# Small bias and gate loads behind the x^T loads, and the K weights in two held halves, in a fused attention and token-MLP kernel

## The chip, the cores and the metric

The kernel runs on one core of one Trainium2 chip. The metric is the device time of one execution in microseconds (us). Before the change the median of five runs is 165.92 us (165.42 to 166.23).

## What is computed

Two mixers read the same x (2048 tokens x 512 features, bf16), and a gate per token blends them:

```
g = sigmoid(sum(x * gate_w))              # one number per token
a = attention(x)                          # 32 heads of 16; each token sees itself and the tokens
                                          # 2, 4, ... 14 back (8 places); then @ wo
h = layernorm(x)                          # over features
u = gelu(einsum("bsd,sf->bdf", h, w1) + b1)   # mixes over the 2048 tokens, F = 1792
b = einsum("bdf,fs->bds", u, w2) + b2         # back to 2048 tokens
out = g * a + (1 - g) * b
```

## The kernel before, in words

All memory on chip is one arena, cut into named regions; `ps` is the accumulator memory of 8 banks. The work has these stages:

1. Head. TensorE warms up on constants (line 546). Token block 0 of x (tiles 0 to 3) is loaded tile by tile, turned on TensorE (line 562), copied out by VectorE (line 574) and ScalarE, and multiplied with Wq, whose four quarters come one by one (line 583), into banks 0 to 3. Between the Q matmuls stand three small transposes (lines 599 to 601): b1, the gate vector and b2 were loaded as rows of 14, 4 and 16 partitions side by side (views `B1R`, `GWR`, `B2R` of the region ROWS) and are turned into columns in bank 7. VectorE copies them out (lines 612 to 614).
2. Projections (line 650), four matmuls of 512 columns each: K and V of block 0, Q and K of block 1, Q and K of blocks 2 and 3, then V of blocks 1 to 3. Blocks 1 to 3 of x^T come by transposing DMAs (`ld_xt`, line 490). ScalarE evacuates the banks, which go round in a ring of seven that leaves out bank 3.
3. Beside this, VectorE takes layer norm statistics (line 682), normalises x (line 696), and forms the attention products Q x K (line 449 is the helper for nearly all of VectorE's work). In the first half of the tokens two additions of such products are done by accumulating DMAs on POOL's queue (`qaddd`, line 737).
4. TensorE sweeps w1 (line 848; two halves of 8 matmuls for each of 14 tiles of F), and between two such halves it forms gate and logit sums over the products (lines 707 and 712). Softmax and the weighted sums over V go on VectorE until near the end.
5. TensorE sweeps w2 (line 875) and adds the output projection of attention (line 884), which needs VectorE's finished blocks `ot0` to `ot7`, two tiles each. ScalarE blends and SP stores.

The order of every engine is set by a planner (`_Sched`): each operation is added with its engine, an estimated duration, what it reads and writes, and a priority; the planner runs through time, takes for each engine the ready operation that can start first, and among equals the one with the longest remaining chain plus its priority. TensorE's operations are chained in the order in which they are written, apart from the logit sums, which go where the planner finds them ready. The waits are then set from the dependences. Loads on one queue are chained in the order in which they are written (`load`, `last_ld`), so a load that waits holds back all that follow it on its queue. SP's queue carries, in this order: x0, Wq0, x2, Wq2, Wk, Wv, x4-7, x^T 1, x8-11, x^T 2, x12-15, x^T 3, the first slab of w1, and then slabs that wait for others. ScalarE's queue carries x1, Wq1, x3, Wq3. POOL's queue carries the gate vector, b1 and b2, later the accumulating DMAs.

Of the kernel before, what the change touches and what calls it, by code (L numbers as in the profile page):

```python
# [5 lines left out]
BF16 = mybir.dt.bfloat16  # L6
# [7 lines left out]
D = 512  # L14
# [4 lines left out]
NST = S // 128  # L19
NFT = F // 128  # L20
# [260 lines left out]
class _Mem:  # L281
# [17 lines left out]
    def view(self, name, dtype, dims, extra=0, p0=0, np_=128):  # L299
        base = self.arena[:].bitcast(dtype)  # L300
        pst = base.ap[0][0]
        esz = mybir.dt.size(dtype)
        o = self.off[name]
        assert o % esz == 0
        return bass.AP(base.tensor, p0 * pst + o // esz + extra, [[pst, np_]] + [list(d) for d in dims])


def bass_gated_mix__sliding_local_dilated__mixer_token_mlp__prompt_kernel(nc, A_x, A_wqkv, A_wo, B_x, B_w1, B_b1, B_w2, B_b2, gate_w, out, dbg=None):
    with contextlib.ExitStack() as es:
        block = es.enter_context(nc.Block())  # L310
        m = _Mem(nc, es)
# [23 lines left out]
        m.region("OUTS", 5 * D * 2)  # L335
        m.region("RP", 32 * 2)
        m.region("GWREP", 4 * 32 * 2)
        m.region("ROWS", 384 * 2)
        m.region("MASK", NW * PAD * 2)
        m.region("SMALL", 2048)  # L340
        m.alias("UT", "WQKV")
# [4 lines left out]
        view = m.view  # L346
# [3 lines left out]
        A = sch.add  # L350

        x2d = A_x[0]
        xv = x2d.rearrange("(t p) d -> p t d", p=128)
        wqkv_v = A_wqkv.rearrange("(dt p) c -> p dt c", p=128)
# [5 lines left out]
        XT = view("XT", BF16, [(S, 4), (1, S)])  # L360
        UT = view("UT", BF16, [(D, NFT), (1, D)])
        WQKV = view("WQKV", BF16, [(3 * D, 4), (1, 3 * D)])
# [37 lines left out]
        IDENT = view("IDENT", BF16, [(1, 128)])  # L400
        ONES = view("ONES", BF16, [(1, 128)])
        RP = view("RP", BF16, [(1, 32)])
        GWREP = view("GWREP", BF16, [(32, 4), (1, 32)])
        MASK = view("MASK", BF16, [(PAD, NW), (1, PAD)], np_=32)
        B1R = view("ROWS", BF16, [(1, 128)], np_=NFT)
        B2R = view("ROWS", BF16, [(1, 128)], extra=128, np_=NST)
        GWR = view("ROWS", BF16, [(1, 128)], extra=256, np_=4)
        so = [0]

        def small(n, dims=None, extra=0):  # L410
# [20 lines left out]
        B1C = small(NFT)  # L431
        B2C = small(NST)
# [5 lines left out]
        def psb(bank):  # L438
            return ps[:, bank, :].bitcast(BF16)

        def sub(ap_, offs, dims):
            return bass.AP(ap_.tensor, ap_.offset + offs, [list(ap_.ap[0])] + [list(d) for d in dims])
# [12 lines left out]
        GELU = "gelu_apprx_tanh_and_others"  # L455
# [6 lines left out]
        A("pool", lambda e: e.memset(sub(KH[0], 0, [(KR, 4), (1, PAD)]), 0.0), 0.2, writes=["kpad"], name="kpad")  # L462
        A("pool", lambda e: e.memset(sub(V5, 0, [(VR, 4), (1, PAD)]), 0.0), 0.2, writes=["vpad"], name="vpad")

        def f_mask(e):
            ins = None
            for w in range(NW):
                if w:
                    ins = e.memset(psub(MASK, 0, 32, w * PAD, [(1, 2 * w)]), NEG)
                if 2 * w < PAD:  # L470
                    ins = e.memset(psub(MASK, 0, 32, w * PAD + 2 * w, [(1, PAD - 2 * w)]), 0.0)
            return ins
# [12 lines left out]
        def load(name, dst, src, nbytes, writes, transpose=False, queue="sp", issue=0.5, order=True, deps=(), after=()):  # L485
            ds = sch.dsem(name)

            def fn(e):
                if transpose:
                    return e.dma_start_transpose(dst, src)  # L490
                return e.dma_start(dst, src)  # L491
            op = sch.dma(queue, fn, nbytes, ds, issue=issue, writes=writes, deps=list(deps) + late_dep[0],
                         after=list(after) + ([last_ld[queue]] if order and queue in last_ld else []), name=name)
            if order:
                last_ld[queue] = op
            return op
# [5 lines left out]
            load(name, WQKV[:, d0:d1, tn * D:(tn + 1) * D], wqkv_v[:, d0:d1, tn * D:(tn + 1) * D], (d1 - d0) * 128 * D * 2, [res])  # L502

        def ld_xt(sb):
            load("xT%d" % sb, XT[:, :, sb * 512:(sb + 1) * 512], x2d[sb * 512:(sb + 1) * 512, :], int(1.4 * 512 * D * 2), ["xt%d" % sb],
                 transpose=True, issue=3.3)

        def ld_first(name, dst, src, nbytes, res, queue):
# [2 lines left out]
        def xq(t, queue):  # L511
            return ld_first("x%d" % t, X[:, t:t + 1, :], xv[:, t:t + 1, :], 131072, ["x%d" % t], queue)

        def wqq(k_, queue):
            return ld_first("wq%d" % k_, WQKV[:, k_:k_ + 1, 0:D], wqkv_v[:, k_:k_ + 1, 0:D], 131072, ["wq%d" % k_], queue)

        for k_ in (0, 2):
            xq(k_, "sp")
            xq(k_ + 1, "act")
            wqq(k_, "sp")  # L520
            wqq(k_ + 1, "act")
        load("wk", WQKV[:, 0:4, D:2 * D], wqkv_v[:, 0:4, D:2 * D], 4 * 128 * D * 2, ["wk"])
        load("gw", GWR, gate_w.rearrange("(t p) -> t p", p=128), 1024, ["gwr"], issue=0.6, queue="pool")
        load("b1", B1R, B_b1.rearrange("(t p) -> t p", p=128), 4096, ["b1r"], issue=0.6, queue="pool")
        load("b2", B2R, B_b2.rearrange("(t p) -> t p", p=128), 4096, ["b2r"], issue=0.6, queue="pool")
        ld_w("wv", 2, 0, 4, "wv")
        for k_ in range(1, 4):
            ld_x(4 * k_, 4)
            ld_xt(k_)

        def ld_w1(j):
            w1ld[j] = load("w1_%d" % j, W1H[j], w1v[:, :, 256 * j:256 * j + 256], S * 256 * 2, [W1R[j]] + (XTALL if j in (3, 4) else []), order=j < 3,
# [18 lines left out]
        def PE(fn, dur, reads, writes, name, prio=0):  # L551
            op = A("pe", fn, dur, reads=reads, writes=writes, after=([chain[0]] if chain[0] is not None else []), name=name, prio=prio)
            chain[0] = op
            return op
# [41 lines left out]
               "q0_%d_%d" % (hb, dt))  # L596

        def f_tb(e):
            e.transpose(out=psb(7)[:, 512:512 + NFT], in_=B1R, identity=IDENT[0:NFT, 0:NFT])  # L599
            e.transpose(out=psb(7)[:, 576:580], in_=GWR, identity=IDENT[0:4, 0:4])  # L600
            return e.transpose(out=psb(7)[:, 544:544 + NST], in_=B2R, identity=IDENT[0:NST, 0:NST])  # L601

        pe_tx(0)
        pe_q0(0, 0)
# [3 lines left out]
        pe_q0(1, 0)  # L608
        pe_q0(1, 1)
        pe_q0(1, 2)  # L610
        PE(f_tb, 0.17, ["b1r", "b2r", "gwr", "ident"], ["b7"], "t_b12")
        A("dve", lambda e: e.tensor_copy(out=GWREP, in_=sub(psb(7), 576, [(1, 4), (0, 32)])), 0.2, reads=["b7"], writes=["gwrep"], name="gwrep", prio=-20)
        A("dve", lambda e: e.tensor_copy(out=B1C, in_=psb(7)[:, 512:512 + NFT]), 0.15, reads=["b7"], writes=["b1c"], name="b1c", prio=-20)
        A("dve", lambda e: e.tensor_copy(out=B2C, in_=psb(7)[:, 544:544 + NST]), 0.15, reads=["b7"], writes=["b2c"], name="b2c", prio=-20)
        pe_q0(2, 3)
        XT0 = ["xt0_%d_%d" % (t, k_) for t in range(4) for k_ in range(2)]

# [23 lines left out]
        def bank_():  # L641
            b = ring[1][ring[0] % len(ring[1])]
            ring[0] += 1
            return b

        def f_proj(tn, dl, sb, bank):
            def fn(e):
                ins = None
                for dt in range(4):
                    ins = e.matmul(ps[:, bank, :], lhsT=sub(WQKV, dt * 3 * D + tn * D + dl, [(4, 128)]),  # L650
                                   rhs=XT[:, dt, sb * 512:(sb + 1) * 512], start=(dt == 0), stop=(dt == 3))
                return ins
            return fn

        WR = {0: ["wq0", "wq1", "wq2", "wq3"], 1: ["wk"], 2: ["wv"]}

        def proj(tn, dl, sb):
            bank = bank_()
            PE(f_proj(tn, dl, sb, bank), 0.87, xt_res(sb) + WR[tn], ["b%d" % bank], "pj%s%d_%d" % ("qkv"[tn], dl, sb))
            evac(tn, dl, sb, bank)  # L660

        for dl in range(4):
            proj(1, dl, 0)
        for dl in range(4):
            proj(2, dl, 0)
        for dl in range(4):
# [3 lines left out]
          reads=["k%d_1" % dl for dl in range(4)], writes=["khalo"], name="khalo")  # L670
        for dl in range(4):
            for tn in range(2):
                for sb in (2, 3):
                    proj(tn, dl, sb)
        ring[0], ring[1] = 0, [0, 1, 2]
        for dl in range(4):
            for sb in range(1, 4):
# [3 lines left out]
        for t in range(NST):  # L681
            A("dve", (lambda t_: lambda e: e.bn_stats(out=ST6[:, t_, :], in_=X[:, t_, :]))(t), 0.67,  # L682
              reads=["x%d" % t], writes=["st%d" % t], name="st%d" % t, prio=-20, after=[extl["dve"]])
# [37 lines left out]
        for h in range(2):  # L721
# [13 lines left out]
            def qaddd(x_, y_, s_, h=h):  # L735
                o_, i_ = (sub(PB[b_], s_ * 4096, [(1, 4096)]) for b_ in (x_, y_))
                qkd[h, s_] = sch.dma("pool", lambda e: e.dma_start(o_, i_, accum_op=ALU.add, max_dma_last_dim=4096), 1800000, sch.dsem("qd%d_%d" % (h, s_)),  # L737
                                     issue=1.3, reads=[PS[y_][s_]], writes=[PS[x_][s_]], name="qd%d_%d" % (h, s_))

            for s_ in range(2):  # L740
                qk(0, bb[0], s_)
# [112 lines left out]
        for ft in range(NFT):  # L854
            bank = MLPB[ft]
            for half in range(2):
                PE(f_ph2(ft, bank, half), 1.735, ["x%d" % t for t in range(8 * half, 8 * half + 8)] + [W1R[ft // 2]], ["b%d" % bank],
                   "ph2_%d_%d" % (ft, half))
            A("act", act(UT[:, ft, :], ps[:, bank, :], AF.Gelu_apprx_tanh, bias=col(B1C, ft)), 0.7,
              reads=["b%d" % bank, "b1c"], writes=["ut%d" % ft] + (["wq0", "wq1", "wq2", "wq3", "wk", "wv"] if ft == 0 else []), name="gel%d" % ft, table=GELU)  # L860
            if ft % 2 == 1 and ft // 2 + 5 <= 6:
                ld_w1(ft // 2 + 5)
        for j in range(8):
# [145 lines left out]
```

## Time and profile before

| | us |
|---|---|
| median of five runs | 165.92 (165.42 to 166.23) |
| the profiled execution's own time | 165.87 |
| its span, first to last instruction | 164.1 |
| TensorE busy | 159.2 |
| VectorE busy | 150.8 |
| ScalarE busy | 75.4 |
| first K matmul (line 650) starts | 9.81 |
| first accumulating DMA issued on POOL | 18.79 |
| first slab of w1 issued on SP | 19.68 |
| logit sums of the first half (line 707) start | 53.14 |

The granted TensorE clock is 1.0 in the whole run. In the profile a line of the timeline gives the start in the span, the time, the engine, the line of the kernel, the operation with output and input, the count, and in brackets how long the engine was idle before it and what released it. Neighbours of one form are merged into one line. "PEld" is TensorE's weight load, which runs beside the matmul before it. A line of the windows gives, for a stretch of time, the busy time and count of PE, PEld, DVE (VectorE), ACT (ScalarE) and POOL, then the granted clock, the share of the 16 DMA engines and the rate in GB/s. The chain is followed back from the last instruction, at each step to what released it.

### The profile page before, as it was taken

Reading aid. Unit: us, or ns where it says so; the run is one execution under the profiler, and the core shown is the slowest. Engines: PE = TensorE matmul, PEld = TensorE weight load, DVE = VectorE, ACT = ScalarE, POOL = GpSimd, SP = SyncE. Lnnn points to the kernel's source line nnn. Section 1 sums busy time; section 2 is a strip of 40 time slices with the busy share of each in tenths; the row PEclk is TensorE's granted clock in tenths of the full one; section 3 lists DMA queues with packets and bytes.
Section 4 is the critical chain, followed back from the end, with each engine's and each line's share of the span. In section 5 each row is a group of like instructions: output and inputs, shape, how many; then the busy total and the mean of one; then the engine's idle time right before and its main releaser. Section 6 shows DMA issues by size and latency. Waiting matters only on the chain.

```text
span 164.1 us, 1993 instructions
## 1 busy us (share of the span) xinstructions
PE 159.2 (97%) x795; PEld 77.3 (47%) x810; DVE 150.8 (92%) x126; ACT 75.4 (46%) x104; POOL 13.7 (8%) x38
## 2 busy tenths in 40 slices
PE   7999999999999999999999999999999999999993
PEld 3755555555544444444444344444444444444641
DVE  0589999999999999999999999999999999999940
ACT  3356677666773599952211669210121111111164
POOL 7000300020000000005000000005001222000000
PEclk9999999999999999999999999999999999999999
DMA  4999999439399287999998974995994899970014
GB/s 160 285 314 268 219 222 216 113 59 187 69 306 279 63 214 212 293 289 265 182 232 241 275 202 138 295 237 148 276 230 149 175 209 191 204 180 35 32 56 136
DMA packets 44696, 32.24 MB, mean 196 GB/s; under 512 B 7952, under 2 KB 42256, under 8 KB 44688
## 3 DMA queue, kind: packets, MB, share of 16 engines
q1 hardware_dynamic: 41360, 22.06, 50.3%
q0 software_dynamic: 2608, 9.45, 29.0%
q10 hardware_dynamic: 720, 0.62, 1.2%
q8 instruction: 6, 0.10, 0.2%
q14 instruction: 2, 0.02, 0.0%
HBM read 18.88 MB, written 2.10 MB: 128 GB/s over the span
## 4 chain that ended last, share of the span: by engine, by line
PE 94%; DMA 3%; ACT 1%; issue 1%; SPq 0%
PE ps L848 29%; PE ps L875 29%; PE ps L650 23%; PE ps L884 8%; DMA arena<-in_A_x_dram 3%; PE ps L583 2%; PE ps L712 1%; ACT arena L452 1%; PE ps L707 1%; SPq L491 0%; PE ps L562 0%; PE ps L599 0%; PE ps L601 0%; PE ps L600 0%
## 5 line engine op out<-in xcount | busy, mean ns | idle before, releaser
L449 DVE TENSOR_TENSOR arena<-arena 128x4096 bf16<-128x4096 bf16 (+8 forms) x79 | 132.1, 1720 | 1.5 <-ACT arena L452 0.5
L875 PE MATMUL ps<-arena 128*128 128x512 bf16 (+2 forms) x234 | 50.0, 366 | 0.2
L452 ACT ACTIVATE arena<-ps,arena 128x512 bf16<-128x512 f32 (+1 forms) x30 | 21.8, 731 | 59.1 <-PE ps L884 40.9
L848 PE MATMUL ps<-arena 128*128 128x512 bf16 x218 | 48.5, 379 | 0.3
L452 ACT ACTIVATE arena<-ps 128x512 bf16<-128x512 f32 (+3 forms) x53 | 33.0, 629 | 18.6 <-PE ps L650 10.8
L650 PE MATMUL ps<-arena 128*128 128x512 bf16 x173 | 38.0, 379 | 0.2
L875 PEld LDWEIGHTS ps<-arena 128*128 128x128 bf16 x238 | 22.8, 98 | 25.9
L848 PEld LDWEIGHTS ps<-arena 128*128 128x128 bf16 x224 | 21.7, 98 | 26.9 <-ACT arena L452 0.7
L650 PEld LDWEIGHTS ps<-arena 128*128 128x128 bf16 x176 | 19.9, 113 | 18.1
L884 PE MATMUL ps<-arena 128*128 128x512 bf16 (+2 forms) x67 | 15.6, 366 | 0.1
L944 ACT ACT_TABLE_LOAD x11 | 14.1, 1283 | 2.9 <-issue 2.7
L780 POOL DMA_DIRECT2D arena<-arena x8 | 4.3, 561 | 74.2 <-DVE arena L449 74.2
L884 PEld LDWEIGHTS ps<-arena 128*128 128x128 bf16 x68 | 6.5, 98 | 7.3
L682 DVE BATCH_NORM_STATS2 arena<-arena 128x6 f32<-128x512 bf16 x16 | 9.9, 678 | 0.0
L452 ACT ACTIVATE arena<-arena 128x16 f32<-128x16 f32 (+5 forms) x10 | 6.8, 679 | 6.1 <-DVE arena L449 6.0
L696 DVE TENSOR_SCALAR arena<-arena 128x512 bf16<-128x512 bf16 x16 | 5.3, 408 | 0.0
L817 POOL DMA_DIRECT2D arena<-arena x3 | 3.6, 1200 | 19.0 <-DVE arena L449 19.0
L574 DVE COPY arena<-ps 128x256 bf16<-128x256 bf16 x4 | 1.2, 292 | 4.2 <-PE ps L562 4.1
L737 POOL DMA_DIRECT2D arena<-arena x2 | 2.5, 1234 | 28.8 <-DVE arena L449 28.8
L583 PE MATMUL ps<-arena 128*128 128x256 bf16 (+1 forms) x27 | 3.8, 286 | 0.4 <-issue 0.2
L924 DVE TENSOR_SCALAR arena<-ps,arena 128x128 bf16<-128x128 f32 x1 | 0.4, 410 | 3.9 <-PE ps L884 3.9
L546 PE MATMUL ps<-const-bfloat16-1.0 128*128 128x512 bf16 (+1 forms) x9 | 2.7, 484 | 0.9 <-PEq L994 0.9
(35 smaller groups left out, 19.1 us busy)
## 6 DMA issues: line engine op xcount, KB each, us to landing
arena<-in_B_w_dram SPq DMA_DIRECT2D x7, 1024.0 KB, 9.3
arena<-in_B_w_dram SPq DMA_DIRECT2D x8, 896.0 KB, 8.2
arena<-arena POOLq DMA_DIRECT2D x5, 1024.0 KB, 9.2
arena<-arena POOLq DMA_DIRECT2D x8, 512.0 KB, 10.6
out_dram<-arena SPq DMA_DIRECT2D x15, 128.0 KB, 1.7
arena<-in_A_x_dram SPq DMA_DIRECT2D x3, 512.0 KB, 4.8
arena<-in_A_wqkv_dram SPq DMA_DIRECT2D x2, 512.0 KB, 6.2
arena<-in_A_wo_dram SPq DMA_DIRECT2D x1, 512.0 KB, 8.4
```

Of the source, the lines that this page charges most:

```text
L449: return lambda e: e.tensor_tensor(out=o_, in0=a_, in1=b_, op=op_)
L452: return lambda e: e.activation(out=o_, in_=i_, func=f_, **kw)
L583: ins = e.matmul(ps[:, dl, c0:c1], lhsT=sub(WQKV, dt * 3 * D + dl, [(4, 128)]), rhs=XT[:, dt, c0:c1], start=(dt == 0 and hb == 0), stop=(d ...
L650: ins = e.matmul(ps[:, bank, :], lhsT=sub(WQKV, dt * 3 * D + tn * D + dl, [(4, 128)]), rhs=XT[:, dt, sb * 512:(sb + 1) * 512], start=(dt = ...
L682: A("dve", (lambda t_: lambda e: e.bn_stats(out=ST6[:, t_, :], in_=X[:, t_, :]))(t), 0.67, reads=["x%d" % t], writes=["st%d" % t], name="s ...
L696: A("dve", (lambda t_: lambda e: e.tensor_scalar(out=X[:, t_, :], in0=X[:, t_, :], scalar1=col(RSTD, t_), scalar2=col(NMR, t_), op0=ALU.mu ...
L780: prev = sch.dma("pool", (lambda d_, s_: lambda e: e.dma_start(d_, s_))(dst, src), 524288, sch.dsem("av%d_%d" % (h, c)), issue=1.0, reads= ...
L817: sch.dma("pool", (lambda o_, i_: lambda e: e.dma_start(o_, i_, accum_op=ALU.add, max_dma_last_dim=4096))(pw(0, 4), pw(4, 4)), 1800000, sc ...
L848: ins = e.matmul(ps[:, bank, :], lhsT=W1H[ft // 2][:, st, 128 * (ft % 2):128 * (ft % 2) + 128], rhs=X[:, st, :], start=(st == 0), stop=(st ...
L875: ins = e.matmul(ps[:, bank, 0:c1 - c0], lhsT=W2S[i // 2][:, ft, 128 * (i % 2):128 * (i % 2) + 128], rhs=UT[:, ft, c0:c1], start=(ft == 0) ...
L884: ins = e.matmul(ps[:, bank, 0:c1 - c0], lhsT=OT[:, i // 2, dl, 128 * (i % 2):128 * (i % 2) + 128], rhs=WO[:, dl, c0:c1], start=False, sto ...
L944: e.preload_act_table_set(want)
```

## The change

The region ROWS shrinks to one row of 128 per partition, and the three vectors lie below each other, b1 from partition 0, b2 from 16, the gate from 32; POOL clears the region first. Their loads move from POOL's queue to SP's, behind x^T 3 and ahead of the first slab of w1. One transpose of the whole 128 x 128 region takes the place of the three; it goes to bank 3 and stands after the second column group (dl = 1) of the Q and K projections of blocks 2 and 3. VectorE's three copies move with it. Wk is loaded in two halves, both of which wait until x0 has landed; for the first two column groups of K, block 0, the matmuls of the first half of the depth are done for both before those of the second. The first accumulating DMAs wait for x^T 3 (`deps=[xtld]`).

```diff
-        m.region("ROWS", 384 * 2)
+        m.region("ROWS", 128 * 2)
...
+        ROWS = view("ROWS", BF16, [(1, 128)])
         B1R = view("ROWS", BF16, [(1, 128)], np_=NFT)
-        B2R = view("ROWS", BF16, [(1, 128)], extra=128, np_=NST)
-        GWR = view("ROWS", BF16, [(1, 128)], extra=256, np_=4)
+        B2R = view("ROWS", BF16, [(1, 128)], p0=16, np_=NST)
+        GWR = view("ROWS", BF16, [(1, 128)], p0=32, np_=4)
...
+        rows0 = A("pool", lambda e: e.memset(ROWS, 0.0), 0.15, name="rows0", prio=-90)
...
+        xld = {}
         for k_ in (0, 2):
-            xq(k_, "sp")
+            xld[k_] = xq(k_, "sp")
             xq(k_ + 1, "act")
             wqq(k_, "sp")
             wqq(k_ + 1, "act")
-        load("wk", WQKV[:, 0:4, D:2 * D], wqkv_v[:, 0:4, D:2 * D], 4 * 128 * D * 2, ["wk"])
-        load("gw", GWR, gate_w.rearrange("(t p) -> t p", p=128), 1024, ["gwr"], issue=0.6, queue="pool")
-        load("b1", B1R, B_b1.rearrange("(t p) -> t p", p=128), 4096, ["b1r"], issue=0.6, queue="pool")
-        load("b2", B2R, B_b2.rearrange("(t p) -> t p", p=128), 4096, ["b2r"], issue=0.6, queue="pool")
+        for k_ in range(2):
+            load("wk%d" % k_, WQKV[:, 2 * k_:2 * k_ + 2, D:2 * D], wqkv_v[:, 2 * k_:2 * k_ + 2, D:2 * D], 2 * 128 * D * 2, ["wk%d" % k_], deps=[xld[0]])
         ld_w("wv", 2, 0, 4, "wv")
         for k_ in range(1, 4):
             ld_x(4 * k_, 4)
-            ld_xt(k_)
+            xtld = ld_xt(k_)
+        load("gw", GWR, gate_w.rearrange("(t p) -> t p", p=128), 1024, ["gwr"], issue=0.4, deps=[rows0])
+        load("b1", B1R, B_b1.rearrange("(t p) -> t p", p=128), 4096, ["b1r"], issue=0.4, deps=[rows0])
+        load("b2", B2R, B_b2.rearrange("(t p) -> t p", p=128), 4096, ["b2r"], issue=0.4, deps=[rows0])
...
         def f_tb(e):
-            e.transpose(out=psb(7)[:, 512:512 + NFT], in_=B1R, identity=IDENT[0:NFT, 0:NFT])
-            e.transpose(out=psb(7)[:, 576:580], in_=GWR, identity=IDENT[0:4, 0:4])
-            return e.transpose(out=psb(7)[:, 544:544 + NST], in_=B2R, identity=IDENT[0:NST, 0:NST])
+            return e.transpose(out=psb(3)[:, 512:640], in_=ROWS, identity=IDENT)
...
-        PE(f_tb, 0.17, ["b1r", "b2r", "gwr", "ident"], ["b7"], "t_b12")
...
-        for dl in range(4):
+        kb0 = [bank_() for dl in range(2)]
+        for k_ in range(2):
+            for dl in range(2):
+                PE(f_proj(1, dl, 0, kb0[dl], 2 * k_, 2 * k_ + 2), 0.44, XT0 + ["wk%d" % k_], ["b%d" % kb0[dl]], "pjk%d_0_%d" % (dl, k_))
+                if k_ == 1:
+                    evac(1, dl, 0, kb0[dl])
+        for dl in range(2, 4):
             proj(1, dl, 0)
...
             for tn in range(2):
                 for sb in (2, 3):
                     proj(tn, dl, sb)
+            if dl == 1:
+                PE(f_tb, 0.06, ["b1r", "b2r", "gwr", "ident"], ["b3"], "t_b12")
...
-                                     issue=1.3, reads=[PS[y_][s_]], writes=[PS[x_][s_]], name="qd%d_%d" % (h, s_))
+                                     issue=1.3, reads=[PS[y_][s_]], writes=[PS[x_][s_]], deps=[xtld], name="qd%d_%d" % (h, s_))
```

The three copies of VectorE that follow the transpose read bank 3 instead of bank 7 and are otherwise the same.

More of the change, by code (lines that the diff above doesn't have):

```diff
@@ L504, in ld_xt @@
         def ld_xt(sb):
-            load("xT%d" % sb, XT[:, :, sb * 512:(sb + 1) * 512], x2d[sb * 512:(sb + 1) * 512, :], int(1.4 * 512 * D * 2), ["xt%d" % sb],
+            return load("xT%d" % sb, XT[:, :, sb * 512:(sb + 1) * 512], x2d[sb * 512:(sb + 1) * 512, :], int(1.4 * 512 * D * 2), ["xt%d" % sb],
                  transpose=True, issue=3.3)
@@ L610, in bass_gated_mix__sliding_local_dilated__mixer_token_mlp__prompt_kernel @@
         pe_q0(1, 2)
-        PE(f_tb, 0.17, ["b1r", "b2r", "gwr", "ident"], ["b7"], "t_b12")
-        A("dve", lambda e: e.tensor_copy(out=GWREP, in_=sub(psb(7), 576, [(1, 4), (0, 32)])), 0.2, reads=["b7"], writes=["gwrep"], name="gwrep", prio=-20)
-        A("dve", lambda e: e.tensor_copy(out=B1C, in_=psb(7)[:, 512:512 + NFT]), 0.15, reads=["b7"], writes=["b1c"], name="b1c", prio=-20)
-        A("dve", lambda e: e.tensor_copy(out=B2C, in_=psb(7)[:, 544:544 + NST]), 0.15, reads=["b7"], writes=["b2c"], name="b2c", prio=-20)
         pe_q0(2, 3)
@@ L644, in bank_, with f_proj @@
             return b
-        def f_proj(tn, dl, sb, bank):
+        def f_proj(tn, dl, sb, bank, d0=0, d1=4):
             def fn(e):
                 ins = None
-                for dt in range(4):
+                for dt in range(d0, d1):
                     ins = e.matmul(ps[:, bank, :], lhsT=sub(WQKV, dt * 3 * D + tn * D + dl, [(4, 128)]),
@@ L653, in f_proj @@
             return fn
-        WR = {0: ["wq0", "wq1", "wq2", "wq3"], 1: ["wk"], 2: ["wv"]}
+        WR = {0: ["wq0", "wq1", "wq2", "wq3"], 1: ["wk0", "wk1"], 2: ["wv"]}
         def proj(tn, dl, sb):
@@ L674, in bass_gated_mix__sliding_local_dilated__mixer_token_mlp__prompt_kernel @@
                     proj(tn, dl, sb)
+            if dl == 1:
+                PE(f_tb, 0.06, ["b1r", "b2r", "gwr", "ident"], ["b3"], "t_b12")
+                A("dve", lambda e: e.tensor_copy(out=GWREP, in_=sub(psb(3), 544, [(1, 4), (0, 32)])), 0.2, reads=["b3"], writes=["gwrep"], name="gwrep", prio=-20)
+                A("dve", lambda e: e.tensor_copy(out=B1C, in_=psb(3)[:, 512:512 + NFT]), 0.15, reads=["b3"], writes=["b1c"], name="b1c", prio=-20)
+                A("dve", lambda e: e.tensor_copy(out=B2C, in_=psb(3)[:, 528:528 + NST]), 0.15, reads=["b3"], writes=["b2c"], name="b2c", prio=-20)
         ring[0], ring[1] = 0, [0, 1, 2]
@@ L859, in bass_gated_mix__sliding_local_dilated__mixer_token_mlp__prompt_kernel @@
             A("act", act(UT[:, ft, :], ps[:, bank, :], AF.Gelu_apprx_tanh, bias=col(B1C, ft)), 0.7,
-              reads=["b%d" % bank, "b1c"], writes=["ut%d" % ft] + (["wq0", "wq1", "wq2", "wq3", "wk", "wv"] if ft == 0 else []), name="gel%d" % ft, table=GELU)
+              reads=["b%d" % bank, "b1c"], writes=["ut%d" % ft] + (["wq0", "wq1", "wq2", "wq3", "wk0", "wk1", "wv"] if ft == 0 else []), name="gel%d" % ft, table=GELU)
             if ft % 2 == 1 and ft // 2 + 5 <= 6:
```

## The prediction

> **What bounds the kernel now.** I read the page first: TensorE's busy row and the chain that ended last.
>
> ```profile
> PE 159.2 (97%) x795; PEld 77.3 (47%) x810; DVE 150.8 (92%) x126; ACT 75.4 (46%) x104; POOL 13.7 (8%) x38
> ...
> PE 94%; DMA 3%; ACT 1%; issue 1%; SPq 0%
> ```
>
> TensorE carries 94% of the chain. The DMA's 3% is one wait of 4.38 us from 1.73, for a tile of x. From the first K matmul on (line 650, 9.81 us) the chain shows only breaks of 0.05 us. So an edit pays only by moving the end of that head, or costs by opening a hole behind it. Next, the timeline of TensorE over the first 10 us (start, busy, and idle before it with its releaser):
>
> ```profile
> 4.89 1.04 PE L583 MATMUL ps<-arena 128*128 128x256 bf16 x8
> 6.16 0.69 PE L562 MATMUL ps<-arena 128*128 128x128 bf16 x8 [0.23 <-DMA arena<-in_A_x_dram]
> 6.88 1.94 PE L583 MATMUL ps<-arena 128*128 128x256 bf16 x16
> 8.76 0.18 PE L599 MATMUL ps<-arena 14*128 14x14 bf16 x1
> ...
> 9.16 0.81 PE L583 MATMUL ps<-arena 128*128 128x512 bf16 x3 [0.18 <-issue]
> 9.81 0.38 PE L650 MATMUL ps<-arena 128*128 128x512 bf16 x1
> ```
>
> Three losses lie there. (1) The 8 Q matmuls from 4.89 step at 0.108 us, so the array was free at 4.89 + 8 x 0.108 = 5.76; the transposes of x tiles 2 and 3 began at 6.15: 0.39 waiting for x. (2) The weight load of the next Q matmul waited for Wq's third quarter: 0.21, in the waits table ("PEld ps L583 <- DMA arena<-in_A_wqkv_dram: 0.2"). (3) The 16 Q matmuls from 6.88 are through at 6.88 + 16 x 0.108 = 8.61; the last Q group's first weight load starts at 8.91 and its first matmul (of four, one record is missing) at 9.81 - 4 x 0.216 = 8.95. The three small transposes cost 0.33, about half of it before the first of them. Then the windows, to see why x comes late (last column GB/s, before it the DMA share):
>
> ```profile
> 3.00:4.00 1.00, 0.83 (x8) 0.59 (x7) 0.00 (x0) 1.00 (x1) 1.00 (x17) 1.00 1.06 361
> 4.00:5.00 1.00, 0.86 (x10) 0.63 (x8) 0.58 (x2) 0.60 (x3) 0.03 (x1) 1.00 1.02 292
> 5.00:6.00 1.00, 0.92 (x8) 0.66 (x7) 0.00 (x0) 0.17 (x1) 0.00 (x0) 1.00 0.68 160
> ```
>
> By 5.0 us 15 + 245 + 361 + 292 = 913 KB had moved, and x0-x3, Wq0-3 together are 1,049 KB. Yet x2 landed at 1.73 + 4.4 = 6.13, x3 at 6.34, Wq2 and Wq3 at 6.8 and 7.0. Whole Wk (issued 2.64), Wv, x4-7 and the three small loads of POOL's queue were in flight beside them, and from 5 to 6 the rate fell to 160.
>
> **Removing the small transposes from the head.** Gain 0.33, as (3).
>
> **The first loads without company.** SP issues x0, Wq0, x2, Wq2, then waits until x0 has landed (0.82 + 2.8 = 3.62), and only then Wk's halves, Wv, x4-7. POOL issues nothing. If 136 KB remain at 5.0 and go at 292 to 361 GB/s, they have moved at 5.4 to 5.5; x2 comes before them, so near 5.2, and Wq3 near 5.8, allowing 0.4 for landing. TensorE would then never wait: 0.39 + 0.21 = 0.60. Bounds: 0 if the dip at 5-6 us has another cause, 0.60 at most, since TensorE is busy up to 5.76. A loss I exclude here: these eight issues stay first on SP and ACT. I take 0.60, because a transfer of the same 128 KB landed in 2.8 to 3.1 us where only others of its kind were in flight, and in 4.4 to 4.8 where Wk was.
>
> **The hold, and who stands behind it on SP.** Wk moves from 2.64 to about 3.7 and 4.15, Wv 4.6, x4-7 5.1, x^T 1 5.6 (before 4.26). Needs: K would start at 9.81 - 0.93 = 8.88; the second half is needed 2 x 0.43 later, 9.75. Whole Wk took 5.7 us under load; that gives 9.4 for the first half, if a half took as long, and 9.85 for the second: bounds 0 and 0.5. I take 0, since at 5.5 the queue ahead of it is empty and 512 KB at 361 GB/s need 1.5 us: landing near 7.5. The Trainium skill ("DMA: Bandwidth & Descriptors", under "Measured (HBM→SBUF, 128 partitions, SWDGE, issued from GpSimd)") speaks against splitting: batch to 1 MiB or more; its fit is a fixed 2.0 us plus bytes/436e3. Wholly in series that is 2 x 2.6 us, and the second half lands near 8.9, still in time; by the row of overlapped 128 KB transfers the fixed part is paid once. Either way 0. Then x^T 1: its issue lasted 6.76 us, to 11.02, against 3.39 and 3.89 for the next two, so it was waiting behind queued bytes; those are no more than before. It landed at 13.06; needed at 8.88 + 8 x 0.867 = 15.8: cover 2.7, against a hold of 1.35. x^T 3 landed at 15.74 + 6.0 = 21.7; needed 9 projections later, 23.6: cover 1.9. Without cover each microsecond late would be a microsecond of TensorE.
>
> **First accumulating DMA behind x^T 3.** POOL issued it at 18.79; now near 21.7. Behind it on POOL is only the second one (34.07), which waits for VectorE anyway. It took 9.2 us: landing 31 instead of 28. VectorE's first overwrite of its source comes at about 38: cover 7. Cost 0.
>
> **Bias and gate loads on SP.** Three issues of 0.4 to 0.5 ahead of W1's first slab: 19.68 becomes about 21. That slab took 11.4 us, beside the accumulation; 33 to 34 is far from its use at 48 less 0.7. The small ones landed in 4.0 to 5.3 us: 24 to 26.5; a row of the DMA view shows that SP's queue (q1) crawls while the accumulation (q0) runs, here from 22 to 23:
>
> ```profile
> q0 software_dynamic: 46, 0.19, 97.3%
> q1 hardware_dynamic: 38, 0.02, 9.5%
> ```
>
> 34 rows and their completions are two such microseconds, so 27 at the latest. They are used at 8.88 + 24 x 0.867 = 29.7: cover 3. Cost 0.
>
> **The full transpose in the projections.** One weight load (0.10 to 0.11) and 128 columns. Nearest row: eight such transposes from 6.16 in 0.69, 0.086 apiece, plus the 0.15 of waits that stood before the old ones, partly under a 0.216 matmul now. The skill ("TensorE: Matmul & The Clock Gate", "Part 4: PE-mode transpose") gives 275 ns in a kernel and 390 alone. By the row 0.1 to 0.25, by the page 0.28 to 0.39, which would eat the 0.33 of (3). I take 0.20: the row is this kernel's own. Bounds 0.06 and 0.4.
>
> **VectorE.** Its three copies leave 9.02-9.48, where it waited 0.32 for ScalarE afterwards, and come back near 30, where it has no idle: +0.45. The interleaved K halves finish the first K tile 0.43 later from K's start, so its first product begins 0.93 - 0.43 = 0.5 earlier. Net about 0. Its deadlines, from single rows of its timeline:
>
> ```profile
> 49.40 2.28 DVE L449 TENSOR_TENSOR arena<-arena 128x4096 bf16<-128x4096 bf16 x1
> ...
> 157.00 0.69 DVE L449 TENSOR_TENSOR arena<-arena 128x1024 bf16<-128x1024 bf16 x1
> ```
>
> The logit sums (line 707, 53.14) need the product ended at 51.68: slack 1.46, less 0.73 leaves 0.7; where the planner puts the sums one half-sweep later, it grows by 1.7 and nothing waits. The last attention block ends at 157.69, needed by the output projection of tile 14 at 156.35 + 16 x 0.216 = 159.8: slack 2.1, less 0.73 leaves 1.4. POOL's memset of the rows and its earlier small memsets lie beside waiting engines: 0.
>
> **Sum.** -0.33 - 0.60 + 0.20 = -0.73. The profiled execution took 165.87 (span 164.1 and 1.77 around it): 165.14. It stands 0.05 below the median 165.92: 165.2.
>
> **Rivals.** *x2 is late anyway* (0.29): the dip at 5-6 us belongs to the transfers themselves. Then only -0.33 + 0.20 = -0.13: 165.8, or with half of the gain 165.5. For it: between 5 and 6 us the two hardware queues still moved 0.07 and 0.09 MB, little of it Wk. Against: the quiet first four loads. That is also the case that the hold doesn't do what it says. *The held queue comes late* (0.15, the slower side): K's second half at its start on TensorE, about 9.75. If it lands as Wv did (3.2 + 6.7, under load) plus a slow start, 4.15 + 7.5 = 11.65, the stall is 1.9 against 0.73: +1.2, 167.1. It decides against the change from a landing at 10.5, and is slower by over 0.3% from 11.0. Against: half the bytes are ahead of it. *More than the sum* (0.04): the new transpose is hidden whole, 165.0. The likeliest, 165.2, has 0.52.
>
> **Chances.** 0.3% is 0.5 us, about what a measurement of this kernel can tell from no change. Faster: 0.52 + 0.04, less the part of the first case above 165.42 (0.05), plus the best of the late-x2 case (0.04): 0.55. Slower: 0.14, the held queue but for a short stall. Within: the rest, 0.31. The likeliest case alone runs from 165.0 to 165.5 by the transpose's bounds. The range goes from 164.9 (0.93 off, no price for the transpose) to 166.2, over the late x2 and a stall of K of about 1 us.
>
> **What would show it.** Right: x2's landing before 5.8 and no idle by DMA before the second group of line 562; the first K matmul near 8.9; one transpose near 30 with a hole of no more than 0.25; breaks of 0.05 elsewhere. Wrong: idle of line 650 released by a DMA of wqkv near 9.7 or of x near 16 or 24; a pause at the transpose for the b loads; VectorE as releaser of line 707 or 884.

## The result, and the profile after

Over 36 executions the changed kernel has a median of 165.49 us (164.69 to 166.47), beside 166.06 for 71 of the kernel before; the ratio is 0.9948, 95% interval 0.9932 to 0.9964, so about 0.86 us (0.60 to 1.13) were gained. Ratios here and below leave out the executions more than 1.5% above the fastest of their kernel, while medians, means and counts above 167 us are over all. The prediction said 165.2, that is 0.72 less. The size is right. This section and the next show that its largest term was not where the time came from.

The profiled execution has a span of 163.5 us against 164.1. TensorE's timeline over the head, as it was shown of before (start, busy, idle before and releaser):

```profile
4.53 1.04 PE L588 MATMUL ps<-arena 128*128 128x256 bf16 x8 [0.38 <-ACT arena L453]
5.40 0.28 PE L567 MATMUL ps<-arena 128*128 128x128 bf16 x2
5.87 0.51 PE L567 MATMUL ps<-arena 128*128 128x128 bf16 x6 [0.19 <-DMA arena<-in_A_x_dram]
6.47 2.80 PE L588 MATMUL ps<-arena 128*128 128x256 bf16 x19
9.11 3.19 PE L649 MATMUL ps<-arena 128*128 128x512 bf16 x14
```

The first K matmul comes at 9.11 instead of 9.81. The Q matmuls now run through without the three small transposes (one group of 19; one record is missing). The transposes of x tiles 2 and 3 (line 567) started at 5.40 (their weight loads at 5.29), but the third still waited for x3 until 5.87, and the Q group behind them for Wq2 until 6.47. The late transpose, from the chain of the changed kernel:

```profile
19.25 10.74 PE ps L649 x49
29.99 0.06 PE ps L604
30.05 0.05 issue
30.10 10.74 PE ps L649 x49
```

It takes 0.06 us of the chain; the 0.05 behind it stands at every 49th matmul in both kernels. From 30 us on everything is 0.65 earlier than before: nothing behind the head gives it back. In this one pair of profiles all of the gain lies in the head. That is a single execution of each, and it misleads, as the runs below show.

### The profile page after: what moved, and what is told of

It is laid out like the page before. It is cut to its first block, busy times and chain, and to the rows that moved or that the text cites. A ratio compares the mean times of both kernels' runs of the same rounds, so it can differ in the third digit from the quotient of the medians.

```text
span 163.5 us, 1989 instructions
## 1 busy us (share of the span) xinstructions
PE 158.6 (97%) x793; PEld 77.0 (47%) x808; DVE 150.7 (92%) x126; ACT 70.1 (43%) x100; POOL 12.0 (7%) x36
## 4 chain that ended last, share of the span: by engine, by line
PE 93%; DMA 3%; ACT 1%; SPq 1%; issue 1%
PE ps L858 30%; PE ps L885 29%; PE ps L649 23%; PE ps L894 8%; DMA arena<-in_A_wqkv_dram 3%; PE ps L588 2%; PE ps L722 1%; ACT arena L453 1%; SPq L494 1%; PE ps L717 1%; PE ps L604 0%
## 5 line engine op out<-in xcount | busy, mean ns | idle before, releaser
L885 PEld LDWEIGHTS ps<-arena 128*128 128x128 bf16 x238 | 22.8, 98 | 25.9
L858 PEld LDWEIGHTS ps<-arena 128*128 128x128 bf16 x224 | 21.6, 98 | 26.9 <-issue 0.8
L649 PEld LDWEIGHTS ps<-arena 128*128 128x128 bf16 x176 | 19.9, 113 | 18.0
L894 PEld LDWEIGHTS ps<-arena 128*128 128x128 bf16 x68 | 6.5, 98 | 7.3
L588 PEld LDWEIGHTS ps<-arena 128*128 128x128 bf16 x28 | 2.9, 114 | 1.0 <-DVE arena L579 0.5
```

What stands on the lines that cost most here:

```text
L588: ins = e.matmul(ps[:, dl, c0:c1], lhsT=sub(WQKV, dt * 3 * D + dl, [(4, 128)]), rhs=XT[:, dt, c0:c1], start=(dt == 0 and hb == 0), stop=(d ...
L858: ins = e.matmul(ps[:, bank, :], lhsT=W1H[ft // 2][:, st, 128 * (ft % 2):128 * (ft % 2) + 128], rhs=X[:, st, :], start=(st == 0), stop=(st ...
L885: ins = e.matmul(ps[:, bank, 0:c1 - c0], lhsT=W2S[i // 2][:, ft, 128 * (i % 2):128 * (i % 2) + 128], rhs=UT[:, ft, c0:c1], start=(ft == 0) ...
L894: ins = e.matmul(ps[:, bank, 0:c1 - c0], lhsT=OT[:, i // 2, dl, 128 * (i % 2):128 * (i % 2) + 128], rhs=WO[:, dl, c0:c1], start=False, sto ...
```

## The experiments

Ratios are to the kernel before, which ran beside each on the same chip, with 95% intervals. The runs were made in four series: the pair of the result, and three series of experiments, each on one chip with the kernel before. The kernel before has a tail: 38 of its 283 executions in the four series took over 167 us (16 of 71, 6 of 62, 10 of 75 and 6 of 75), and its mean is 166.17 where its median is 165.97. Landing times come from the one profiled execution of each run.

**The hold alone.** The kernel before with Wk in two held halves, and with the interleaved K halves (the edit is shown in part):

```diff
-        load("wk", ...4 rows of WQKV..., ["wk"])
+        for k_ in range(2):
+            load("wk%d" % k_, ...2 rows..., ["wk%d" % k_], deps=[xld[0]])
```

> The kernel before with one part of the change alone: Wk in two halves that wait for x0, with the interleaved K halves; bias and gate loads stay on POOL's queue and the three small transposes in the head. Theory (Wk and what follows it crowd the first loads): x3 lands near 5.8 and Wq2 near 6.4, as in the changed kernel, and the first K matmul starts near 9.4, so -0.4 us against before (ratio 0.9976). Rival (the three small loads on POOL's software queue are what slows the first loads): x2 still lands near 6.1, Wq2 near 6.8, first K matmul near 9.8, ratio 1.000.

Measured: 1.0016 (0.9996 to 1.0037), 5 of 22 above 167, mean 166.75. x2 landed at 5.7 and Wq2 at 6.6, between the two theories, and the first K matmul started at 9.78. The profiled execution (span 167.9) is one of the long ones and brought something else: x^T 3 landed at 26.45, and TensorE waited 2.0 us for it by the waits view.

**The change without the hold.** `deps=[xld[0]]` removed from the changed kernel.

> The changed kernel with the hold taken away: Wk's halves are issued at once; the small loads stay behind x^T 3. Theory (Wk crowds the first loads): x2 and Wq2 late again, 6.1 and 6.8; only the 0.3 of the small transposes is kept, first K matmul near 9.5, ratio to before 0.9985. Rival (POOL's small loads slowed the first loads): x2 near 5.0, Wq2 near 6.4 as in the changed kernel, first K matmul near 9.1, ratio 0.995.

Measured: 0.9967 (0.9948 to 0.9985) in 9 executions, mean 165.47. x2 landed at 5.1, x3 at 5.4, Wq2 at 6.2, earlier than with the hold. My theory that Wk crowds the first loads fell. The rival, POOL's small loads, stood for the moment.

**A longer hold.** Wk's halves wait for x2 (`deps=[xld[2]]`).

> The changed kernel with a longer hold: Wk's halves wait for x2 instead of x0, so they are issued near 5.1 and 5.5 and everything behind them on SP's queue 1.4 us later. Theory (what is left of the head's waits, 0.36 for x3 and 0.27 for Wq2 in the changed kernel, comes from Wk's first half beside them): x3 near 5.5, Wq2 near 5.9, K ready to start near 8.7; Wk's first half lands near 8.2 to 8.5, so no stall: -0.3 against the changed kernel, ratio to before 0.993. Rival (the held queue comes late): Wk's halves land after 8.9 and 9.3 and TensorE waits at K; as the changed kernel or slower, up to 1.0, with idle released by a DMA of wqkv before the K matmuls.

Measured: 1.000 (0.9983 to 1.0017), mean 166.13. Even with Wk and all that follows it held back until x2 had landed, x2 came at 5.6 and Wq2 at 6.3. The windows of this run show the queue running dry behind the hold (the last two columns are DMA share and GB/s):

```profile
5.00:6.00 1.00, 1.00 (x6) 0.68 (x5) 0.00 (x0) 0.16 (x1) 0.00 (x0) 1.00 0.41 137
6.00:7.00 1.00, 1.00 (x13) 0.86 (x12) 0.21 (x1) 0.10 (x1) 0.00 (x0) 1.00 0.17 20
```

K itself didn't wait. But x^T 1 landed at 7.67 + 8.3 = 15.97 with 16.5 as its need, and x^T 3 at 18.36 + 5.9 = 24.26 with 24.3: the cover of 2.5 and 1.9 us that the changed kernel has in its profile is used up. The held queue comes late, as the rival said, with x^T rather than K as the transfer at the edge; that it is this that costs the 0.7 us on average, the one profile does not show.

**Eight transposes in place of one.**

```diff
-            return e.transpose(out=psb(3)[:, 512:640], in_=ROWS, identity=IDENT)
+            for r_ in range(8):
+                ins = e.transpose(out=psb(3)[:, 512:640], in_=ROWS, identity=IDENT)
+            return ins
```

> The changed kernel with the whole-region transpose done eight times over in place of once: the price of one by itself. By the row of the head's transposes (0.086 each) seven more cost 0.6 us, by the Trainium skill's 275 ns 1.9 us, and by the 390 ns of a transpose alone 2.7 us. First K matmul at 9.1 as in the changed kernel; ratio to the kernel before 0.9985, 1.006 or 1.011.

Measured: 0.9992 (0.9972 to 1.0011). In its chain:

```profile
30.23 0.45 PE ps L605 x8
```

In this chain seven more cost 0.45 - 0.06 = 0.39, 0.056 each, which is about a quarter of a 512-column matmul at 0.216: the transpose in this running stream costs the time of its 128 columns and no more. By the times the seven cost somewhat more: the mean is 166.00 against 165.45 for the changed kernel over two other series, 0.55 with a standard error of 0.09. The 275 and 390 ns that the Trainium skill's "TensorE: Matmul & The Clock Gate" gives ("Part 4: PE-mode transpose") are much too large as a price in this stream by either measure (the profile records each transpose as 0.219 us long, but they overlap). My 0.20 for one was too large by the chain's 0.06.

**The change without the wait for x^T 3.** `deps=[xtld]` removed.

> The changed kernel without the accumulating DMA's wait for x^T 3. Theory (the held SP queue issues x^T 3 some 0.3 us later, and the accumulation, issued near 18.3, starves it, as in the run with the hold alone, where x^T 3 landed at 26.45 and TensorE stood still for about 3 us): in a good part of the executions x^T 3 lands after 24 and TensorE waits 1 to 3 us; several runs above 167 us, mean ratio to before above 1.000. Rival (the wait does nothing, as the prediction had it): as the changed kernel, no run above 167, ratio 0.995.

Measured: 1.0035 (1.0004 to 1.0066), 12 of 22 above 167, up to 169.99, mean 167.37, which is 1.3 above the kernel before beside it. Without the wait that I had booked at zero, the change is a loss. The accumulating DMA and x^T 3 in the timelines of this run, each in its own:

```profile
18.76 1.32 POOL L747 DMA_DIRECT2D arena<-arena  x1 [16.54 <-DVE arena L450]
```

```profile
17.32 4.64 SPq L493 DMA_TRANSPOSE arena<-in_A_x_dram  x1
```

From 24 to 25 us the DMA view has this one line for the queues, of POOL's software queue; SP's queue with x^T 3 moved no packet at all:

```profile
q0 software_dynamic: 48, 0.20, 98.4%
```

x^T 3 landed 9.7 us after its issue began, at 27.0, and not after 5.9 as with the wait. The DMA view's lines for it, the first of this run, the second of the changed kernel:

```profile
arena<-in_A_x_dram SPq DMA_TRANSPOSE x1, 9.7
arena<-in_A_x_dram SPq DMA_TRANSPOSE x1, 5.9
```

TensorE's timeline names the DMA of x as what ended its idle time:

```profile
27.11 7.64 PE L649 MATMUL ps<-arena 128*128 128x512 bf16 x28 [2.82 <-DMA arena<-in_A_x_dram]
```

The windows show what it did to TensorE (first pair after the window's length: TensorE busy; the column after POOL is the granted clock):

```profile
24.00:25.00 1.00, 0.29 (x2) 0.00 (x0) 0.96 (x6) 0.97 (x4) 0.00 (x0) 1.00 0.98 197
25.00:26.00 1.00, 0.00 (x0) 0.00 (x0) 1.00 (x1) 0.25 (x2) 0.00 (x0) 1.00 0.99 197
26.00:27.00 1.00, 0.00 (x0) 0.00 (x0) 0.96 (x3) 0.00 (x0) 0.00 (x0) 0.82 1.34 259
27.00:28.00 1.00, 0.89 (x3) 0.36 (x4) 1.00 (x4) 0.00 (x0) 0.00 (x0) 0.50 0.84 202
28.00:29.00 1.00, 1.00 (x4) 0.37 (x3) 1.00 (x5) 0.00 (x0) 0.00 (x0) 0.50 1.15 347
29.00:30.00 1.00, 1.00 (x3) 0.29 (x2) 1.00 (x5) 0.60 (x1) 0.00 (x0) 0.50 1.19 295
```

TensorE idles for 2.8 us. Its granted clock falls to half while it still idles (0.82 for the window from 26 to 27, so from about 26.6) and stays there until 30.0: seven matmuls at 0.427 instead of 0.216, 1.5 us more. This stall of 2.8 us costs 4.3.

**The kernel before with that wait alone** (the lines that set `xtld` are left out here).

```diff
-                issue=1.3, reads=[PS[y_][s_]], writes=[PS[x_][s_]], name=...
+                issue=1.3, reads=[PS[y_][s_]], writes=[PS[x_][s_]], deps=[xtld], name=...
```

> The kernel before with the wait for x^T 3 alone. Theory (the kernel before sometimes meets the same collision, which is its tail of runs above 167 us: 16 of 71 and 6 of 62, against none of 36 of the changed one): the tail goes, the median stays; no run above 167, median ratio 1.000, mean ratio 0.997 to 0.998. Rival (the tail has another cause): tail as before, ratio 1.000.

Measured: 0.9989 (0.9973 to 1.0005); none of 22 above 167, against 10 of 75 of the kernel before beside it; median 165.85 against 165.95, mean 165.76 against 166.10. The tail goes and the median moves by 0.1, as the theory had it. The interval of the ratio contains 1, so the tail is the evidence. Taken alone, none of 22 would come up by luck about once in 15 times; but over all runs, the kernels with this wait were above 167 in 1 of 243 executions (that one with the longer hold), and the kernels without it in 38 of 283, 5 of 22 and 12 of 22.

**The small loads back on POOL's queue** at the start, without the hold, with the late transpose and the wait.

> The changed kernel without the hold, and with the three small loads back on POOL's queue at the start; the one late transpose stays. Theory (it is the small loads on POOL's software queue that hold up x2 to Wq3): x2 near 6.1, Wq2 near 6.8 again, ratio to before 0.998 to 0.9985 (the small transposes' 0.24 saved, and the tail). Rival (the small loads are innocent, the transfers' own timing varies): x2 near 5.1, Wq2 near 6.2 as without the hold, ratio 0.996.

Measured: 0.9978 (0.9963 to 0.9994), mean 165.62. x2 landed at 5.4, Wq2 at 6.3: early, with the small loads in place. The ratio was near the theory's and the landings were not, so the theory of the software queue lost its mechanism; the same kernel again, below, had 0.9959.

**The small loads on SP's queue, right behind Wq2.**

> The changed kernel without the hold, and with the three small loads on SP's queue right behind Wq2, ahead of Wk. Theory (the software queue is what hurts, not the small loads as such): x2 near 5.1, Wq2 near 6.2, ratio 0.996; Wk 1.3 us later on SP, landing near 8.6 to 9.0, at the edge of its use. Rival (any small load so early hurts): x2 and Wq2 late, 6.0 and 6.8, ratio 0.998.

Measured: 0.9971 (0.9954 to 0.9988), mean 165.46. x2 at 5.8, Wq2 at 6.5: late in the landing, and no slower for it. So, as far as one profile of each can tell, neither where the small loads go nor whether Wk is held decides when x2 comes. Four more runs on one chip, to compare among themselves:

**The changed kernel again.**

> The changed kernel once more, on one chip with the next three, for a comparison among them. So far its runs have a mean of 165.43 us. Theory now (three gains: the tail of x^T 3 collisions, about 0.3; the small transposes out of the head, 0.2; the small loads off POOL's queue, perhaps 0.15): mean 165.4 to 165.5, no run above 167, the same as without the hold. Rival (the hold is what makes it faster): 0.2 or more below the kernel without the hold.

Measured: 0.9956 (0.9937 to 0.9975), mean 165.47.

**Without the hold again.**

> The changed kernel without the hold once more (9 runs had a mean of 165.47 us). Theory (the hold is worth nothing): mean within 0.1 us of the changed kernel in the same job. Rival (the hold clears the way for the first loads): slower by 0.2 or more.

Measured: 0.9966 (0.9945 to 0.9987), mean 165.57: 0.10 above the changed kernel, with a standard error of 0.11. The theory stands as far as that can tell.

**The small loads early on POOL's queue again.**

> The kernel without the hold and with the three small loads early on POOL's queue once more (22 runs had a mean of 165.62 us). Theory (small loads on POOL's queue cost the first loads a little): 0.1 to 0.2 us slower than without the hold in the same job. Rival (they cost nothing): within 0.05.

Measured: 0.9959 (0.9940 to 0.9977), mean 165.52: not slower than without the hold, which speaks for the rival.

**Wk in one transfer, not held, K in the plain order;** small loads late, one transpose, wait for x^T 3.

> The changed kernel with Wk in one transfer again, not held, and with K in the plain order: what is left of the change is the small loads behind x^T 3, the one late transpose, and the wait for x^T 3. Theory (hold and split are worth nothing): mean as the changed kernel, 165.4 to 165.5, ratio to before 0.995 to 0.997; x^T 3 lands some 0.5 us earlier than with the hold. Rival (the split or the hold matters): slower than the changed kernel by 0.2 or more.

Measured: 0.9971 (0.9956 to 0.9987), mean 165.59: 0.12 above the changed kernel, with a standard error of 0.10, between theory and rival. x^T 3 landed at 22.0, against 21.9 and 23.0 in the two profiles of the changed kernel.

Over all series together the means are: changed 165.45 (58 executions), without the hold 165.54 (31), with the small loads early on POOL's queue as well 165.57 (44), with the wait alone 165.76 (22), before 166.17 (283). The standard error of each of the first four is 0.05 to 0.07. Of the variants named here none is faster than the changed kernel, and only the wait alone is clearly slower.

## Why the prediction was right in size, and wrong in its main step

The changed kernel's second profile shows what the head gained, because in it x2 happened to land as late as in the profile of before, and the Q matmuls before it ran at the same pace (8 in 1.04):

```profile
4.83 1.04 PE L588 MATMUL ps<-arena 128*128 128x256 bf16 x8
6.23 0.68 PE L567 MATMUL ps<-arena 128*128 128x128 bf16 x8 [0.36 <-DMA arena<-in_A_x_dram]
6.92 2.80 PE L588 MATMUL ps<-arena 128*128 128x256 bf16 x19
9.56 1.67 PE L649 MATMUL ps<-arena 128*128 128x512 bf16 x7
```

The wait for x is there, undiminished. K starts at 9.56 against 9.81: 0.25 less, and that is the small transposes. All the profiles agree: from the start of this Q group to the first K matmul it is 2.93 to 2.97 us in the three with the small transposes in the head, and 2.63 to 2.68 in the eleven without.

- *"Removing the small transposes from the head. Gain 0.33."* Right: of 0.34 in the chain around them, 0.05 of issue is left, so 0.29.
- *"The first loads without company. I take 0.60."* This step failed. Landing from issue, in us, in the fourteen profiled executions:

| | x2 | Wq2 |
|---|---|---|
| not held, small loads on POOL (before, wait alone, small loads on POOL twice) | 4.4, 3.5, 3.7, 3.9 | 4.6, 3.8, 4.1, 4.8 |
| held, small loads on POOL | 4.0 | 4.4 |
| not held, small loads elsewhere (four runs) | 3.4, 4.1, 4.4, 4.1 | 4.0, 4.3, 4.6, 4.3 |
| held, small loads late (changed twice, longer hold, eight transposes, no wait) | 3.3, 4.4, 3.9, 4.2, 4.3 | 4.2, 4.7, 4.1, 4.5, 4.6 |

  x2 lands 3.3 to 4.4 us after its issue with any of these queues: the two profiles of the changed kernel (3.3 and 4.4) span the whole range. I read one late landing in one execution as the work of its neighbours, and inferred from it a gain that an edit could fetch. My reason was that loads landed in 2.8 to 3.1 us beside their own kind and in 4.4 to 4.8 beside Wk. But the first two loads of each queue landed in 2.5 to 3.2 us in all fourteen profiles, and the next two in 3.3 to 5.0, also where Wk was held until x2 had landed (3.9 to 4.3): what goes with the landing time is the place in the queue. The dip to 160 GB/s belongs to that one execution: of the other thirteen, twelve moved 251 to 339 from 5 to 6 us, x2 landing late in some of them all the same, and the thirteenth is the longer hold with its empty queue. (The sum of 136 KB left at 5.0 also took every byte moved till then for one of the first eight loads.) Of "x2 is late anyway", my first rival, this much holds: no part of the change makes it earlier. Why its landing varies stays open. From the means, holding Wk and moving the small loads are together worth 165.57 - 165.45 = 0.12 with a standard error of 0.07, not told apart from nothing.
- *"The full transpose. I take 0.20."* Too dear: 0.06 in the chain. With the first term, -0.29 + 0.06 = -0.23; the means give 165.55 - 165.76 = -0.21, with a standard error of 0.07 (165.55 is the mean of the 119 executions that have the late transpose and the wait but no hold).
- *"First accumulating DMA behind x^T 3. Cost 0."* It costs nothing (VectorE waits once for an accumulating DMA, 0.4 us in one profile and 0.2 in the other, and TensorE never waits for that), but it is the largest gain: 166.17 - 165.76 = 0.41 in the mean, or 0.34 against the executions beside it, most of it from the tail. I had quoted the row in which the accumulation leaves SP's queue a tenth of the bytes, and the profile of before has x^T 3 landing at 21.7 with the accumulation's packets from 21. I asked what the wait delays and not what it protects. That the tail of the kernel before is such a collision is shown by the wait's taking it away; no execution of that tail was profiled.
- *The hold and SP's queue.* K didn't wait, as said: Wk's halves landed at 7.2 and 8.4 in the first profile after, 3.8 and 4.5 us from their issues and overlapping. The fit that the prediction took from the Trainium skill stands in the page's section "Anatomy of one DMA — SWDGE (gpsimd) path" and is for the software queue, while Wk goes on SP's hardware queue; the estimate from it, 2.6 us for each half in series, was not what happened. What the hold delays is x^T 3, and without the wait that goes with a collision that is common and no longer rare: x^T 3 was issued 3.05 us ahead of the accumulation in the profile of before (38 of 283 executions above 167), 2.04 with the hold alone (5 of 22 above 167) and 1.44 in the change without the wait (12 of 22). The small loads' part in the last was not tried without the hold. Also, "each microsecond late would be a microsecond of TensorE" is too little, since 2.8 cost 4.3. The hold needs the wait, and by itself it brings nothing that could be measured.
- *VectorE.* The sums went one half-sweep later (after 32 matmuls of the w1 sweep, line 858, instead of 24; the traces hold 31 and 23 of them), as foreseen, and nothing waited for it. ScalarE's table loads fell from 11 to 7, which it had no need of.

So the sum was -0.33 - 0.60 + 0.20 = -0.73, and the terms are about -0.29 + 0.06 for the transposes, -0.41 for the wait, and -0.1, within its error, for the rest: -0.72 between the means. That the two sums agree is chance: the largest term of the prediction is nearly absent, and a gain that it did not have fills the gap.

## What to carry to other kernels

A wait seen in one execution is worth its length only if it is there in the next one: profile the unchanged kernel twice before pricing a wait of a few tenths. A wait that is added to a transfer can be a gain: look up what that transfer shares the engines with, and how near the other one's landing is to its need. Compare the spread of runs as well as the medians: here the tail had a cause of its own, which a wait of one transfer for another took away.

## What the runs showed of the hardware

TensorE's pace in the head differs from execution to execution, though the granted clock reads 1.00 there. The first eight Q matmuls in the run with the longer hold, as against 1.04 above:

```profile
4.88 1.76 PE L588 MATMUL ps<-arena 128*128 128x256 bf16 x8
```

They step at 0.21 us instead of 0.108: the array is at half pace until about 6.4 us there, about 5.6 in the run with eight transposes, and is at full pace from 3.5 on in the first profile after. The Trainium skill's "TensorE: Matmul & The Clock Gate" ("Part 1: The HAM clock gate") has this as a window of 3.4 us that runs freely, so that the change to full rate comes at a different place in each run; the profiles agree, over some 3 us. The changed kernel's first profile is 0.36 ahead at the first Q matmul, its eight transposes before it taking 0.61 instead of 1.01; in its second profile they take 1.01 and that matmul starts at 4.83, against 4.89 before, so this lead is not the work of the change. When the pace changes late, TensorE is busy until x2 has landed and there is no wait to save. The same part of the page wants an idle window of about that length before the rate falls again. Here less was enough. In the change without the wait the granted clock fell about 2.3 us after TensorE went idle, and in the hold alone, whose wait was only 2.0 us, it fell as TensorE had just started again; both times it stayed at 0.50 for 3.4 us, from 26.6 to 30.0.

The software queue's accumulation and a transposing load do not share the engines evenly: 0.20 MB against nothing from 24 to 25 us in the run without the wait.
